# Sparse attention and Fourier mixing: the first attention without conversion, and Strassen in half of the first batch's second layer

## The chip, the cores and the metric

The kernel runs on one core of a Trainium2 chip. The metric is the device time of one execution in microseconds (us). Engines are named as in the profile: PE is the matrix engine (PEld its weight loads), DVE the vector engine, ACT the scalar engine, POOL the general-purpose engine, SP the engine whose queue issues most DMAs.

## What is computed

Attention over 4 batches, 8 heads, 768 tokens, head size 64, with a local window and a summary of every block of 32 tokens; then a Fourier mix, a normalization and two dense layers. Cut to what matters:

```python
k_sum = k.reshape(B, H, nb, 32, D).max(axis=3)          # 24 block summaries
v_sum = v.reshape(B, H, nb, 32, D).mean(axis=3)
local = where(|i - j| < 16, (q @ k.T) / 8, -1e9)
block = (q @ k_sum.T) / 8 + log(32)
a = softmax(concatenate([local, block], -1))
x = (a @ concatenate([v, v_sum], 2))                     # to (4, 768, 512)
u = x + real(fft(fft(x, axis=1), axis=2))
un = (u - mean(u)) / sqrt(var(u) + 1e-6)
out = u + relu(un @ w_ch1) @ w_ch2                       # 512 x 2048, 2048 x 512
```

The two weight matrices arrive as 64-bit floats, which the kernel reads as pairs of 32-bit words and converts on the chip.

## The kernel before

`_main_program` (line 487) handles batches 0 to 3 one after the other: attention (`gen_attention`, 788) in four pairs of heads, Fourier mix (`gen_fourier`, 972), first dense layer (`gen_hidden`, 1086) and second (`gen_out`, 1133). The dense layers go in two halves of four of the eight 128-wide blocks j of each half of the hidden dimension, in the order hidden 0, out 0, hidden 1, out 1. Attention and Fourier mix of the next batch are woven into the dense layers of the present one by `drive` (1220), which steps several generators in turn; a priority is given to the Fourier mix. `_general_program` (78 to 416) runs only if a flag found at the end says that the fast program's numbers were out of bounds.

Strassen's method (in Winograd's form) computes a product of two 2x2 block matrices with 7 block products in place of 8. `_left_sums` (473) and `_right_sums` (480) make the sums that it needs, four each. `gen_hidden` uses it in all batches (line 1101, 384 columns an instruction, right sums of the normalized input, left sums of the weights). `gen_out` uses it for batches 1 to 3 (line 1167, 256 columns, left sums of h in tiles of tag "s"), and for batch 0 the plain product (line 1142, 512 columns). The matmuls are fp32, which PE does in two instructions each.

The weights: `plan` (827) lists pieces (matrix, block j, stage that must have been issued first). `load_raw` (833) loads their words, three ahead, `convert` (847) turns 128x512 of them into floats with five DVE operations (L857, L858, L862, L864 and a product by `tt`, L560) and two ACT operations (L859, L860), `make` (870) does two pieces for a block, for the first matrix its left sums too, and stores the result to DRAM, from where the later batches fetch it (`get_w1` 908, `get_w2` 915). For the second matrix batch 0 stores four parts; batch 1 fetches these, makes the four right sums on DVE and stores parts 1 to 6, and batches 2 and 3 fetch all seven.

The first attention (batch 0 only) is "wide": queries are taken 64 at a time against 96 keys (`wide_scores` 685, L695, L699), the exponentials are multiplied by a mask `wide` of 128 x 768 (the band, and which tokens exist; rows 96 to 119 are the 24 block summaries), and `wide_values` (713, L718) multiplies by `vw`, a tile with a row of values for each of 96 keys, the block sums below, and a column of counts that gives the softmax's sum. `load_wide_values` (625) loads it, with one DMA for a head (two for the first, where the rows before token 0 are left at zero). `prepare` (656) transposes k and q of a pair on PE (L668) and copies them to SBUF (L670 for batch 0, L678 for others), `block_sums` (584) adds up v over each block for two pairs at once (POOL chains by `gtt`, L563; DVE for batch 1, L560 and L605), and `sum_values` (705) brings the sums to `vw` by way of PE (L709) and ACT (L710). The raw data of the block sums are in the tiles of tag "s" as long as weights are being made.

`fetch` (545, L547) issues a DMA on SP's queue, in program order until batch 0's dense layers. What SP waits for holds all that is behind it. DMAs of SP and ACT share eight semaphores in turn, so that each waits for the landing of the one eight places before it.

In `gen_fourier` DVE first makes sums and differences of the two halves of the tokens, for each parity (`sd`, `zw`, `fg`, with small copies to `zq` and the edges of `fg`, L990, L994, L997), PE then multiplies by tables (L1014), and DVE and ACT normalize. `keep_busy` (946, L952) has PE multiply a few idle products while DVE makes the first fold. `tc.issue_after(marks[...])` holds an instruction in the schedule until the marked one.

Of the kernel before, what the change touches and what calls it, by code (L numbers as in the profile page):

```python
# [422 lines left out]
def _tables(S, DM):  # L423

    g = _general_consts(S, DM)
    nb = S // BLOCK

    r, i, c = np.arange(96)[:, None, None], np.arange(S // QB)[None, :, None], np.arange(QB)[None, None, :]
    tok = QB * i - W + r
    wide = np.ones((P, S // QB, QB), dtype=np.float32)  # L430
    wide[0:96] = (r > c) & (r < c + 2 * W) & (tok >= 0) & (tok < S)
    count = np.zeros((P, 1), dtype=np.float32)
    count[0:96], count[96:96 + nb] = 1.0, BLOCK

    r, i, c = np.arange(64)[:, None, None], np.arange(nb)[None, :, None], np.arange(BLOCK)[None, None, :]
    tok = BLOCK * i - W + r
    near = (r > c) & (r < c + 2 * W) & (tok >= 0) & (tok < S)
    near = np.concatenate([near, near]).astype(np.float32)


    sel = np.zeros((4 * nb, 2, 2, 2, 32), dtype=np.float32)
    half = np.zeros((2, 2, 32, 2), dtype=np.float32)
    for h in range(2):
        half[:, h, :nb, h] = 1.0
        for e in range(2):
            for pair in range(2):
                for n in range(nb):
                    sel[(2 * pair + e) * nb + n, pair, e ^ h, h, n] = 1.0

    fs = np.ascontiguousarray(np.moveaxis(g["fs"], 2, 0))  # L450


    fd = g["fd"].reshape(P, 6, DM // 2)
    n = DM // 4
    odd = fd[:, 1, 1:n].copy()
    odd[0] = 0.0
    fm = np.concatenate([fd[:, 0, 0:n + 1], fd[:, 3, 0:n], odd, fd[:, 4, 0:n], fd[:, 1, 0:n + 1]], axis=1)
    fm = np.ascontiguousarray(fm)
    return dict(wide=wide, near=near, sel=sel.reshape(4 * nb, 2, P), half=half.reshape(P, 2), count=count, fs=fs,
                fd=g["fd"], fm=fm, ident=g["ident"])  # L460
# [26 lines left out]
def _main_program(ctx, tc, q, k, v, moe_w_ch1, moe_w_ch2, out):  # L487
# [36 lines left out]
    wide = bpool.tile([P, NC, 2, S], FP, tag="h", name="wide").rearrange("p j h s -> p (j h s)")  # L524
    wide = wide[:, 0:NQ * QB].rearrange("p (n c) -> p n c", n=NQ)
    near = cpool.tile([P, 2, NB2, BLOCK], FP, name="near")
    sel = cpool.tile([4 * nb, 2, P], FP, name="sel")
    half_of = cpool.tile([P, 2], FP, name="half")
    count = cpool.tile([P, 1], FP, name="count")
    rebias = cpool.tile([P, 1], FP, name="rebias")  # L530
# [52 lines left out]

    def block_sums(b, gg):

        f = BLOCK // 4
        n = f * D
        if done_weights:
            raw = room(f"vb_{b}_{gg}")
            raw = [raw[0:4 * nb, n * i:n * (i + 1)] for i in range(4)]  # L590
        else:

            raw = [bpool.tile([P, NC, P], FP, tag="s", bufs=5, name=f"vb_{b}_{gg}_{i}").rearrange("p n t -> p (n t)")
                   [0:4 * nb] for i in range(4)]
        for i in range(4):
            fetch(out=raw[i], in_=v[b, 4 * gg:4 * gg + 4].rearrange("h (n f) d -> (h n) (f d)", f=BLOCK)
                  [:, n * i:n * (i + 1)])
        vb = spool.tile([4 * nb, D], FP, tag="vbs", bufs=2, name=f"vbs_{b}_{gg}")

        add = tt if b == 1 else gtt  # L600
        add(raw[0], raw[0], raw[1], ADD)
        add(raw[2], raw[2], raw[3], ADD)
        add(raw[0], raw[0], raw[2], ADD)
        if b == 1:
            nc.vector.tensor_reduce(out=vb, in_=raw[0].rearrange("p (f d) -> p d f", d=D), op=ADD, axis=AX.X)  # L605
        else:
            while f > 2:
                f //= 2
                gtt(raw[0][:, 0:f * D], raw[0][:, 0:f * D], raw[0][:, f * D:2 * f * D], ADD)
            gtt(vb, raw[0][:, 0:D], raw[0][:, D:2 * D], ADD)  # L610
        sums[b, gg] = vb

# [7 lines left out]
    def load_values(b, g):  # L620
        if g % 2 and following(b, g, 1):
            block_sums(*divmod((b * NP + g + 1) // 2, NP // 2))
        (load_wide_values if is_wide(b) else load_narrow_values)(b, g)

    def load_wide_values(b, g):

        vw = wide_vw(g)
        for e in range(2):
            off = v[b, 2 * g + e].offset
            parts = [(W, WK, 0, NQ), (0, W, 1, NQ)] if (b, g, e) == (0, 0, 0) else [(0, WK, 0, NQ)]  # L630
            for r0, r1, i0, i1 in parts:
                fetch(out=vw[r0:r1, e, i0:i1, 0:D],
                                  in_=bass.AP(v.tensor, off + (QB * i0 - W + r0) * D,
                                              [[D, r1 - r0], [QB * D, i1 - i0], [1, D]]))

    def load_narrow_values(b, g):
# [3 lines left out]
        if g < 2 and is_wide(b - 1):  # L640
            nc.gpsimd.memset(vw[WK:P, :, D:D1], 1.0)
        for e in range(2):
# [42 lines left out]
    def wide_scores(b, g):  # L685
# [3 lines left out]
        for half in range(2):  # L689
# [10 lines left out]
            for e in range(2):  # L700
                nc.scalar.activation(out=p[:, e, n0:n1], in_=ps[e], func=AF.Exp, scale=SC)
                tt(p[:, e, n0:n1], p[:, e, n0:n1], wide[:, n0:n1], ALU.mult)
        return p

    def sum_values(b, g):

        ps = abank([P, 2, D], f"vs_{b}_{g}")
        for e in range(2):
            nc.tensor.matmul(ps[WK:P, e], sel[:, g % 2, D * e:D * e + 32], sums[b, g // 2], start=True, stop=True)  # L709
        nc.scalar.copy(out=wide_vw(g)[WK:P, :, :, 0:D],  # L710
# [43 lines left out]
    def values(b, g, p, pm, x):  # L754
        vw = vw_bufs[g % 2]
        ps = abank([P, D], f"vs_{b}_{g}")
        nc.tensor.matmul(ps, sel[:, g % 2, :], sums[b, g // 2], start=True, stop=True)
        tt(vs[:, :, 0:D], ps[:, None, :].to_broadcast([P, 2, D]),
# [29 lines left out]
    def gen_attention(b):  # L788
        x = bpool.tile([P, NST, DM], FP, tag="x", bufs=2, name=f"x_{b}")
        x_of[b] = x  # L790
        for g in range(NP):
            p = (wide_scores if is_wide(b) else scores)(b, g)
            yield
            if is_wide(b):
                sum_values(b, g)
            else:
                sum_scores(b, g, p[1])
            n1, n2 = following(b, g, 1), following(b, g, 2)
# [3 lines left out]
            if n1:  # L802
                with tc.issue_after(marks["last av"]) if early else ExitStack():
                    prepare(*n1)

            for n in {(0, 1): (), (0, 2): (2,), (0, 3): (2, 3)}.get((b, g), (3,)):
# [4 lines left out]
            if not early:  # L811
                if is_wide(b):
                    wide_values(b, g, p, x)
                else:
                    values(b, g, *p, x)
            if n2:
                load_values(*n2)
            if (b, g) == (0, 0):
                load_raw(2)
            yield  # L820
# [5 lines left out]

    plan = [(1, 0, None), (1, 1, ("fold", 0)), (1, 2, ("mx", 0)), (2, 0, ("mx", 0)), (1, 3, ("h", 0, 0)), (2, 1, ("mx", 0)),
            (2, 2, ("mx", 0)), (2, 3, ("mx", 0)), (1, 4, ("h", 0, 1)), (1, 5, ("h", 0, 2)), (1, 6, ("h", 0, 3)),
# [41 lines left out]
    def make(f, j):  # L870
# [10 lines left out]
        if f == 1:  # L881
            _left_sums(tt, lambda i: wv[:, i])
        else:

            to, wv = to[:, 0:4], wv[:, 0:4]
        yield
        stores.append((to, wv))
# [27 lines left out]
    def get_w2(b, j):  # L915
# [3 lines left out]
        wt[2, b, j] = w  # L919
        if b == 1:  # L920
            fetch(out=w[:, 0:4], in_=dw2[j][:, 0:4])
# [50 lines left out]
    def gen_fourier(b):  # L972
# [10 lines left out]
        for par in range(2):  # L983
# [5 lines left out]
            keep_busy(b, par, zw)  # L989
            nc.vector.tensor_copy(out=zq[:, par], in_=zw[:, :, Q])  # L990
            nc.vector.memset(fg[:, :, Q:Q + 1], 0.0)
            tt(fg[:, :, 1:Q], zw[:, :, 1:Q], zw[:, :, HD - 1:Q:-1], ADD)
            tt(fg[:, :, Q + 1:HD], zw[:, :, 1:Q], zw[:, :, HD - 1:Q:-1], SUB)
            nc.vector.tensor_copy(out=fg[:, :, 0:DM:HD], in_=zw[:, :, 0:DM:HD])  # L994
            tt(fg[:, :, HD + 1:HD + Q], zw[:, :, HD + 1:HD + Q], zw[:, :, DM - 1:HD + Q:-1], SUB)
            tt(fg[:, :, HD + Q:DM - 1], zw[:, :, HD + 1:HD + Q], zw[:, :, DM - 1:HD + Q:-1], ADD)
            ins = nc.vector.tensor_copy(out=fg[:, :, DM - 1:DM], in_=zw[:, :, HD + Q:HD + Q + 1])  # L997
            fgs.append(fg)
# [134 lines left out]
    def gen_out(b, c):  # L1133
        x, h = x_of[b], wt["h", b]
        js = range(NC * c, NC * (c + 1))
        if b == 0:

            for t in range(NST):
# [7 lines left out]
                tt(x[:, t, :], ps, x[:, t, :], ADD)  # L1146
                if NC * (c + 1) == NJ:
                    fetch(out=out[b, P * t:P * (t + 1), :], in_=x[:, t, :])
            issued.add(("o", b, c))
# [46 lines left out]
    load(0, 0)  # L1196
    fetch(out=wide, in_=dr["wide"].ap())
    nc.scalar.dma_start(out=count, in_=dr["count"].ap())
# [3 lines left out]
    for kt, km in zip(kt_bufs, km_bufs):  # L1202
        nc.vector.memset(kt[:, 0:W], 0.0)
        nc.vector.memset(kt[:, W + S:], 0.0)
        nc.vector.memset(km, 0.0)
    nc.vector.memset(vw_bufs[0][0:W, 0, 0:D], 0.0)
    block_sums(0, 0)
    load_values(0, 0)
    load(0, 1)
    prepare(0, 0)  # L1210
    for vw in vw_bufs:
        nc.gpsimd.tensor_copy(out=vw[:, :, D], in_=count.to_broadcast([P, nb]))
    load_values(0, 1)
# [35 lines left out]
    attn = gen_attention(1)  # L1249
    drive((gen_fourier(0), 4, 600), (first(weights, 66), 12, 0), (first(attn, 5), 1, 0))  # L1250
    for b in range(B):

# [66 lines left out]
```

## Time and profile before

| | us |
|---|---|
| median of 6 runs | 848.32 (846.68 to 849.58) |
| profiled execution | 848.45 |
| its span, first to last instruction | 846.7 |
| granted PE clock, mean | 0.987 |
| first attention, to the first fold on DVE | 0 to 57.3 |
| Fourier mix of batch 0, to the first X of layer 1 | 57.3 to 104.5 |
| out, second half of batch 0, with the Fourier mix of batch 1 | 241.2 to 304.6 |
| batches 1, 2, 3 start their layer 1 at | 304, 503, 696 |

The profile's busy shares are in the section on the prediction. The 40 slices of the span show the early part as the only place where PE is not full, and the clock low there (tenths, each slice 21 us):

```profile
PE   5979998999999999999999999999999999999997
DVE  2487996987976443544357943443338953532352
PEclk8969999999999999999999999999999999999999
DMA  9998685979523273444943235403411326205001
```

How to read its lines: a group of instructions gives line, engine, operation, tiles written and read, shape, count, then busy time and mean duration of one in ns, then the idle time before them and what ended it. The chain of waits follows the last instruction back: each row has a start, a length and what took it. A window row gives, for each engine, busy us and in brackets the number of instructions, then the granted clock, the DMA share and GB/s.

### The profile page before, as it was taken

Reading aid. Unit: us, or ns where it says so; the run is one execution under the profiler, and the core shown is the slowest. Engines: PE = TensorE matmul, PEld = TensorE weight load, DVE = VectorE, ACT = ScalarE, POOL = GpSimd, SP = SyncE. Lnnn points to the kernel's source line nnn. Section 1 sums busy time; section 2 is a strip of 40 time slices with the busy share of each in tenths; the row PEclk is TensorE's granted clock in tenths of the full one; section 3 lists DMA queues with packets and bytes.
Section 4 is the critical chain, followed back from the end, with each engine's and each line's share of the span. In section 5 each row is a group of like instructions: output and inputs, shape, how many; then the busy total and the mean of one; then the engine's idle time right before and its main releaser. Section 6 shows DMA issues by size and latency. Waiting matters only on the chain.

```text
span 846.7 us, 14497 instructions
## 1 busy us (share of the span) xinstructions
PE 814.0 (96%) x6006; PEld 568.9 (67%) x6006; DVE 480.4 (57%) x1115; ACT 230.4 (27%) x473; POOL 37.0 (4%) x44
## 2 busy tenths in 40 slices
PE   5979998999999999999999999999999999999997
PEld 4847754545556555787667875688667885786586
DVE  2487996987976443544357943443338953532352
ACT  3524666552721113122232103120321112101100
POOL 3200002003000200001000000000000000000000
PEclk8969999999999999999999999999999999999999
DMA  9998685979523273444943235403411326205001
GB/s 215 230 275 166 156 230 183 260 246 294 205 81 131 75 268 135 120 108 152 249 103 102 73 132 217 111 24 78 171 59 57 113 65 246 87 1 217 1 27 53
DMA packets 102858, 120.94 MB, mean 143 GB/s; under 512 B 50592, under 2 KB 83584, under 8 KB 102784
## 3 DMA queue, kind: packets, MB, share of 16 engines
q1 hardware_dynamic: 102240, 119.77, 48.8%
q8 instruction: 49, 0.80, 0.4%
q10 hardware_dynamic: 544, 0.17, 0.1%
q14 instruction: 25, 0.20, 0.1%
HBM read 95.80 MB, written 24.12 MB: 142 GB/s over the span
## 4 chain that ended last, share of the span: by engine, by line
PE 80%; DVE 9%; ACT 6%; DMA 3%; issue 1%; SPq 0%; ACTq 0%; DVEq 0%
PE hx L1101 18%; PE ox L1167 13%; PE o L1142 9%; PE hz L1101 9%; PE oz L1167 7%; PE hy L1101 4%; PE y L1014 4%; PE oy L1167 3%; DVE x L560 3%; PE sc L735 2%; PE mx L963 1%; ACT qt L678 1%; ACT kt L678 1%; PE sc L695 1%; PE unt L1079 1%
## 5 line engine op out<-in xcount | busy, mean ns | idle before, releaser
L1101 PE MATMUL hx<-u,w 128*128 128x384 f32 x512 | 186.1, 492 | 8.5 <-ACT h L1111 6.5
L1101 PEld LDWEIGHTS hx<-u,w 128*128 128x128 f32 x512 | 94.4, 190 | 75.2 <-ACT h L1111 9.8
L1101 PE MATMUL hz<-u,w 128*128 128x384 f32 x256 | 93.2, 486 | 0.0
L1142 PE MATMUL o<-w,h 128*128 128x512 f32 x192 | 84.9, 595 | 0.0
L1101 PEld LDWEIGHTS hz<-u,w 128*128 128x128 f32 x256 | 48.6, 190 | 33.9 <-ACT h L1118 0.2
L1167 PE MATMUL ox<-w,s 128*128 128x256 f32 x288 | 69.0, 381 | 0.4 <-DVE x L560 0.3
L1167 PE MATMUL oz<-w,s 128*128 128x256 f32 x288 | 68.7, 379 | 0.0
L1167 PE MATMUL ox<-w,h 128*128 128x256 f32 x288 | 66.9, 380 | 0.0
L1142 PEld LDWEIGHTS o<-w,h 128*128 128x128 f32 x192 | 35.7, 190 | 41.9 <-issue 39.9
L560 DVE TENSOR_TENSOR x<-ox,x 128x256 f32<-128x256 f32 x72 | 30.3, 423 | 55.7 <-PE ox L1167 55.7
L1167 PEld LDWEIGHTS ox<-w,h 128*128 128x128 f32 x288 | 54.4, 190 | 8.3
L1167 PEld LDWEIGHTS ox<-w,s 128*128 128x128 f32 x288 | 53.9, 190 | 8.4 <-DVE x L560 1.2
L1167 PEld LDWEIGHTS oz<-w,s 128*128 128x128 f32 x288 | 54.4, 190 | 7.2
L560 DVE TENSOR_TENSOR h<-hx,h 128x384 f32<-128x384 f32 x32 | 17.8, 556 | 71.5 <-PE hx L1101 71.5
L560 DVE TENSOR_TENSOR h<-hy,h 128x384 f32<-128x384 f32 x32 | 17.8, 556 | 57.2 <-PE hy L1101 54.0
L1111 ACT COPY h<-hx 128x384 f32<-128x384 f32 x32 | 15.3, 478 | 121.7 <-PE hx L1101 110.0
L1101 PE MATMUL hy<-u,w 128*128 128x384 f32 x128 | 46.5, 486 | 0.0
L1127 ACT ACTIVATE h<-hx 128x384 f32<-128x384 f32 x32 | 15.7, 491 | 78.9 <-PE hx L1101 78.8
L1014 PE MATMUL y<-fs,fold 128*128 128x193 f32 x192 | 37.1, 336 | 0.0
L679 DVE TENSOR_REDUCE km<-kt 128x24 f32<-128x768 f32 x16 | 15.2, 952 | 38.5 <-ACT kt L678 25.1
L1014 PEld LDWEIGHTS y<-fs,fold 128*128 128x128 f32 x192 | 31.1, 189 | 7.6 <-issue 6.0
L1101 PEld LDWEIGHTS hy<-u,w 128*128 128x128 f32 x128 | 24.3, 190 | 17.0
(125 smaller groups left out, 1105.4 us busy)
## 6 DMA issues: line engine op xcount, KB each, us to landing
w<-dw SPq DMA_DIRECT2D x40, 896.0 KB, 5.2
words<-in_moe_w_ch_dram SPq DMA_DIRECT2D x32, 512.0 KB, 6.6
vw<-in_v_dram SPq DMA_DIRECT2D x47, 192.0 KB, 5.8
dw<-w SPq DMA_DIRECT2D x8, 896.0 KB, 7.1
kn<-in_k_dram SPq DMA_DIRECT2D x16, 384.0 KB, 4.8
qn<-in_q_dram SPq DMA_DIRECT2D x16, 384.0 KB, 5.4
vb<-in_v_dram SPq DMA_DIRECT2D x32, 192.0 KB, 5.5
out_dram<-x SPq DMA_DIRECT2D x24, 256.0 KB, 2.6
```

Of the source, the lines that this page charges most:

```text
L560: nc.vector.tensor_tensor(out=out, in0=in0, in1=in1, op=op)
L678: nc.scalar.copy(out=dst[D * e:D * (e + 1), s:S:2], in_=ps[D * s:D * (s + 1)])
L679: nc.vector.tensor_reduce(out=km[:, 0:nb], in_=kt[:, W:W + S].rearrange("p (n f) -> p n f", f=BLOCK), op=ALU.max, axis=AX.X)
L695: nc.tensor.matmul(ps[e][0:WK, n - n0, :], kt[rows, QB * n:QB * n + WK], qt[rows, QB * n:QB * (n + 1)], start=True, stop=True)
L735: nc.tensor.matmul(ps[h][r:r + 64, i, :], kt[rows, o:o + 64], qt[rows, o:o + BLOCK], start=True, stop=True)
L963: nc.tensor.matmul(out, y[:, g], table, start=True, stop=last, skip_group_check=True)
L1014: nc.tensor.matmul(y, fgs[par][:, st, P * g:P * (g + 1)], fs[par][:, g % 2, st, :], start=(st == 0), stop=(st == HT - 1))
L1101: nc.tensor.matmul(ps, w[:, a, kk, :], u[:, r, kk, :], start=start and kk == 0, stop=stop and kk == 1, skip_group_check=True)
L1111: nc.scalar.copy(out=c11, in_=X)
L1127: nc.scalar.activation(out=c21, in_=X, func=AF.Relu)
L1142: nc.tensor.matmul(ps, h[:, n, hf, P * t:P * (t + 1)], wt[2, b, j][:, 2 * hf:2 * hf + 2, :], start=(n, hf) == (0, 0), stop=(n, hf) == (NC ...
L1167: nc.tensor.matmul(ps, left[a][:, n, :], wt[2, b, j][:, r, :], start=start and n == 0, stop=stop and n == NC - 1, skip_group_check=True)
```

## The change

It has eight parts.

1. The mask becomes one pattern of 128 x 64, broadcast over the tiles of queries; what is out of range is handled by zeroed value rows and zero counts (now 128 x 12). Both are loaded by ACT's queue. `vw` is loaded with three DMAs a head.
2. Two products of zeros on PE stand before the first transposes, after a memset on POOL.
3. `block_sums` of batch 0's first two pairs are done pair by pair (48 rows). Those of batch 1's first two pairs move from DVE to POOL; those of its last two stay on DVE and move behind the Fourier mix of batch 0.
4. The sums of pair 0 are brought to `vw` after the transposes of pair 1, no longer before them.
5. The first piece of the weights waits for the fold of batch 0, and so leaves the first attention; `load_raw(2)` moves ahead of a pair's value loads.
6. In `gen_out` the second half of batch 0 goes by Strassen, as in later batches.
7. For that, batch 0 makes the right sums of blocks 4 to 7 of the second matrix and stores all seven parts, and batch 1 fetches them.
8. Small copies in `gen_fourier` (three for each parity, all batches) go from DVE to ACT, and the mark "fold" moves to the product that is now last.

```diff
@@ tables
-    wide = np.ones((P, S // QB, QB), dtype=np.float32)
-    wide[0:96] = (r > c) & (r < c + 2 * W) & (tok >= 0) & (tok < S)
-    count = np.zeros((P, 1), dtype=np.float32)
-    count[0:96], count[96:96 + nb] = 1.0, BLOCK
+    wide = np.ones((P, QB), dtype=np.float32)
+    wide[0:96] = (r > c) & (r < c + 2 * W)
+    count = np.zeros((P, S // QB), dtype=np.float32)
+    count[0:96] = (QB * i - W + r >= 0) & (QB * i - W + r < S)
+    count[96:96 + nb] = BLOCK
@@ block_sums
-    def block_sums(b, gg):
+    def block_sums(b, gg, g=None):
+        rows, heads = (4 * nb, slice(4 * gg, 4 * gg + 4)) if g is None else (2 * nb, slice(2 * g, 2 * g + 2))
...
-        add = tt if b == 1 else gtt
+        add = tt if (b, gg) == (1, 1) else gtt
@@ load_values
-        if g % 2 and following(b, g, 1):
+        if g % 2 and following(b, g, 1) and (b, g) != (1, 1):
             block_sums(*divmod((b * NP + g + 1) // 2, NP // 2))
@@ load_wide_values
-            parts = [(W, WK, 0, NQ), (0, W, 1, NQ)] if (b, g, e) == (0, 0, 0) else [(0, WK, 0, NQ)]
+            parts = [(W, WK, 0, 1), (0, WK, 1, NQ - 1), (0, WK - W, NQ - 1, NQ)]
@@ wide_scores
-                tt(p[:, e, n0:n1], p[:, e, n0:n1], wide[:, n0:n1], ALU.mult)
+                tt(p[:, e, n0:n1], p[:, e, n0:n1], wide[:, None, :].to_broadcast([P, NQ // 2, QB]), ALU.mult)
@@ gen_attention
-            if is_wide(b):
+            if not is_wide(b):
+                sum_scores(b, g, p[1])
+            elif g:
                 sum_values(b, g)
-            else:
-                sum_scores(b, g, p[1])
...
                     prepare(*n1)
+            if (b, g) == (0, 0):
+                sum_values(b, g)
...
+            if (b, g) == (0, 0):
+                load_raw(2)
             if n2:
                 load_values(*n2)
-            if (b, g) == (0, 0):
-                load_raw(2)
@@ plan, make, get_w2, gen_out
-    plan = [(1, 0, None), (1, 1, ("fold", 0)), ...
+    plan = [(1, 0, ("fold", 0)), (1, 1, ("fold", 0)), ...
...
+        elif j < NC:
+            to, wv = to[:, 0:4], wv[:, 0:4]
         else:
-            to, wv = to[:, 0:4], wv[:, 0:4]
+            _right_sums(tt, lambda i: wv[:, i])
...
-        if b == 1:
+        if b == 1 and j < NC:
             fetch(out=w[:, 0:4], in_=dw2[j][:, 0:4])
...
-        if b == 0:
+        if (b, c) == (0, 0):
@@ gen_fourier
-            nc.vector.tensor_copy(out=zq[:, par], in_=zw[:, :, Q])
+            nc.scalar.copy(out=zq[:, par], in_=zw[:, :, Q])
...
-            nc.vector.tensor_copy(out=fg[:, :, 0:DM:HD], in_=zw[:, :, 0:DM:HD])
+            nc.scalar.copy(out=fg[:, :, 0:DM:HD], in_=zw[:, :, 0:DM:HD])
...
-            ins = nc.vector.tensor_copy(out=fg[:, :, DM - 1:DM], in_=zw[:, :, HD + Q:HD + Q + 1])
+            nc.scalar.copy(out=fg[:, :, DM - 1:DM], in_=zw[:, :, HD + Q:HD + Q + 1])
@@ start
-    fetch(out=wide, in_=dr["wide"].ap())
+    zeros = bpool.tile([P, 7, 2, S2], FP, tag="u", name="zeros").rearrange("p a k n -> p (a k n)")[:, 0:640]
+    nc.gpsimd.memset(zeros, 0.0)
+    ps = bank([P, 512], "warm")
+    for i in range(2):
+        nc.tensor.matmul(ps, zeros[:, 512:640], zeros[:, 0:512], start=True, stop=True)
+    nc.scalar.dma_start(out=wide, in_=dr["wide"].ap())
...
-    nc.vector.memset(vw_bufs[0][0:W, 0, 0:D], 0.0)
-    block_sums(0, 0)
+    for g in range(2):
+        nc.vector.memset(wide_vw(g)[0:W, :, 0, 0:D], 0.0)
+        nc.vector.memset(wide_vw(g)[64:WK, :, NQ - 1, 0:D], 0.0)
+    block_sums(0, 0, 0)
     load_values(0, 0)
     load(0, 1)
+    block_sums(0, 0, 1)
     prepare(0, 0)
@@ main schedule
     drive((gen_fourier(0), 4, 600), (first(weights, 66), 12, 0), (first(attn, 5), 1, 0))
+    block_sums(1, 1)
```

## The prediction

> **What bounds the kernel now.** I read the busy shares first, then the costliest groups, then the chain of waits, then stages.
>
> ```profile
> PE 814.0 (96%) x6006; PEld 568.9 (67%) x6006; DVE 480.4 (57%) x1115; ACT 230.4 (27%) x473; POOL 37.0 (4%) x44
> PE 80%; DVE 9%; ACT 6%; DMA 3%; issue 1%; SPq 0%; ACTq 0%; DVEq 0%
> L1142 PE MATMUL o<-w,h 128*128 128x512 f32 x192 | 84.9, 595 | 0.0
> L1167 PE MATMUL ox<-w,s 128*128 128x256 f32 x288 | 69.0, 381 | 0.4 <-DVE x L560 0.3
> ```
>
> TensorE (PE) is busy nearly always and 80% of the chain, so a saved PE instruction counts wherever PE does not pause. L1142 is the plain second layer of batch 0, L1167 the Strassen one of the later batches. Their means overlap, so I take rates from runs on the chain (start us, us, what):
>
> ```profile
> 283.34 21.46 PE o L1142 x50
> 742.37 3.45 PE ox L1167 x16
> ```
>
> A 512-wide instruction costs 21.46/50 = 0.429 us, a 256-wide one 3.45/16 = 0.216 us. Windows then show whether PE and DVE have room where batch 0's second half runs (PE busy, PEld, DVE, ACT, POOL, clock, DMA share, GB/s):
>
> ```profile
> 240.00:250.00 10.00, 10.00 (x31) 4.95 (x29) 9.12 (x16) 1.03 (x3) 0.00 (x0) 1.00 0.12 34
> 260.00:270.00 10.00, 10.00 (x62) 7.83 (x62) 8.17 (x27) 0.00 (x0) 0.00 (x0) 1.00 0.27 93
> 290.00:300.00 10.00, 10.00 (x25) 4.46 (x24) 1.38 (x2) 0.00 (x0) 3.18 (x4) 1.00 0.13 45
> ```
>
> PE is full there; DVE is not (the six windows from 240 to 300 hold 37.0 us of DVE work, 23 idle). The first attention is the opposite. The chain begins and ends in waits there:
>
> ```profile
> 9.34 8.73 DMA kn<-in_k_dram
> 18.21 4.81 PE qk L668 x48
> ...
> 52.90 0.60 DVE vb L560
> 53.65 0.92 DVE vbs L605
> ...
> 55.04 0.60 DVE words L862
> 55.74 0.57 DVE words L864
> 56.78 0.60 DVE w L560
> 57.37 1.68 DVE fold L560
> ```
>
> Pair 1's keys land at 18.1 while PE has stood still; the transposes behind run at half clock (the windows from 16 to 22 grant 0.50). At the end, DVE finishes block sums of batch 1 and a weight conversion before it may start the first fold. Three queue rows, for the place of pair 2's keys (start, time held, what):
>
> ```profile
> 16.83 1.65 SPq L547 DMA_DIRECT2D vw<-in_v_dram  x2
> 18.57 4.18 SPq L547 DMA_DIRECT2D kn<-in_k_dram  x1
> 21.43 1.27 POOL L563 TENSOR_TENSOR vb<-vb,vb 96x512 f32<-96x512 f32 x1 [4.34 <-DMA vb<-in_v_dram]
> ```
>
> **The change part by part.**
>
> Strassen in the second half of batch 0's second layer. It removes 6 tiles x 8 products of 512 columns; fp32 takes 2 instructions each: 96 x 0.429 = 41.2 us. It adds 3 x 7 x 4 x 2 = 168 of 256 columns: 168 x 0.216 = 36.2. **-5.0 us.** The groups' means (0.442 over 192 from 84.9; (69.0+68.7+66.9)/864 = 0.237) would give 42.4 - 39.8 = -2.6: the other bound. I take the chain's rates, since those are spans of consecutive work. DVE pays 12 left sums at 0.69 (a 128x512 operation), 21 updates at 0.42 and loses 6 at 0.69: +13 us, hidden by the 23 idle ones. Without that cover PE would wait; the same layout in batches 1 and 2 makes PE wait 0.3 us in all (the L1167 row). The right sums of four weight blocks (16 x 0.42 = +6.7) fall into 210 to 240, where DVE is busy 22.8 of 30: 7.2 idle, a tight fit. If they spill, the fold of batch 1, at 241, is late by what spills (0 to 2). The larger stores (+393 KB four times) go on queues with a share of 0.4 to 0.8.
>
> In batch 1 the same 16 sums and four stores vanish. PE lost at most 0.4 us there against batch 2: -0.2 (0 to -0.4).
>
> Start of the first attention. Less is loaded before pair 1's keys: the mask goes from 384 to 33 KB, the block-sum data of the first group is halved (-0.39 MB): 0.74 MB at the 0.24 MB/us of these windows is 3 us, so landing at 15 instead of 18.1. PE's pause before it then falls from 3.5 us (13.66 to 17.14) to about 1.4. But the value sums of pair 0 now come after these transposes: PE copies 0.4 to PSUM, ACT spreads them in 1.43, and the value products wait, 1.8 us that lay beside other work before. Scores of pair 1 (24.39 before) start at 15 + 4.8 + 1.8 + 1.44 = 23.0 at half clock, at 21.1 at full (2.9 for the transposes): **about -2**. The two warm-up products cost four instructions at 0.86, 3.4 us, after a memset on the idle POOL, ahead of keys that land at 4.78: nothing, as the next thing late is pair 1's load; without that cover a few tenths. Four memsets on DVE and the count copies on POOL lie in idle time too.
>
> Pair 2's keys. On SP they used to be issued at 18.57, behind two value loads. Now there stand before them: four block-sum loads of 96 KB for pair 1 (each waits for the sums of pair 0 on POOL, which free its buffers), four loads for batch 1, of which the last waits for the third sum of pair 1's chain on POOL, and six value loads instead of two. SP also holds each DMA until the one issued eight places earlier has landed, as the program's semaphores go round (so SP waits 1.7 us on `sel`, which ACT loads), and keys 2 wait for a load of batch 1. POOL's first chain (six sums of 48x512; 6 us in the 96x512 rows) ends about 16, the third sum of the second about 21; add the 5.5 us median landing of such loads: keys 2 leave about 25.5 at the latest and land after 4.8 (their median), at 30.3; with landings of 3 us, at 28. I take 29.5. PE, ready at about 26.6, starts them 0.9 later than the 28.60 of before. So start and keys together: **+0.9**, from -2.0 (landing in time) to +4 (30.8 and half a clock, which cost 4.81 - 2.9 = 1.9 at pair 1).
>
> The Trainium skill (TensorE: Matmul & The Clock Gate, Part 1) says an idle window of about 3.4 us halves the clock, and its closing table asks for no pause over 3 us. Its rule would charge nothing for my pause of 2.9 and some 1.7 more for one half a microsecond longer. The 3.48 us pause above is followed by 0.50, which agrees.
>
> End of the first attention. Block sums of batch 1 (0.60, 0.92) and conversion steps (0.60, 0.57, 0.60) leave DVE's last stretch, 3.29 us. The limit becomes the last value products, 54.71 by the records, plus a reciprocal and a product: fold at 55.4 instead of 57.3: **-1.9** (0 to -3.3).
>
> Fold stage. Four left sums (4 x 0.41) and six small copies, which go to an idle ACT, leave it, so the first mixed half comes 1.7 sooner. But the conversion removed from the attention returns behind it (+4.9), against -0.6 copies, -2.7 block sums moved on, -0.9 conversion moved on, -1.2 end of attention, +0.9 batch-1 scores: +0.4 on a DVE busy for 40.7 of the 45.5 us up to layer 1. I take **0** (-1.7 to +0.4). In the first layer 1, DVE takes the late block sums (2.7; the first tiles wait for DVE and ACT there: 0 to +2), and ACT's first copy of a product stands ahead of four q copies of 0.5 (-2 to 0): **0**. Extra mask broadcasts and batch 0's later value loads (6 per pair) I cost at nothing, covered by PE's work from 28 to 50.
>
> Sum: -5.0 - 0.2 + 0.9 - 1.9 + 0 = -6.2. The profiled execution is 848.45 (span 846.7 and 1.75 around it), the median 848.32: 842.25, stated as **842.2 us**.
>
> A rule against the change: the Trainium skill (DMA: Bandwidth & Descriptors, Anatomy of one DMA) gives each DMA a fixed 2.0 us whatever its size, in a fit for another issuing path. By it the 14 more DMAs through eight places would cost at most an estimated 14 x 2/8 = 3.5 us, and the sum would be 845.7. Here 1 KB of `half` took 6.83 us to land in a full queue, so queueing, not the fixed part, sets it.
>
> **The rivals.**
>
> *The early part pays in full.* Keys 2 land by 26.6 (-2.0 instead of +0.9), and the fold's 1.7 reaches layer 1. For: less is loaded, and small loads may land in 3 us. Against: the waits on SP. 842.2 - 2.9 - 1.7 = 837.6.
>
> *SP's queue loses it all (slower).* If the second block-sum data of pair 1 land at 21 to 23, as batch 1's did (the POOL row: 21.43, next load 22.89), POOL's third sum ends at 25.5, batch 1's load lands at +7.2, the median of the early loads, 32.7, and keys 2 at about 36.5: 7.9 later than the use at 28.60, plus 1.9 of half clock: +9.8 in place of +0.9: 851.1. It decides once keys 2 land after about 34: slower than before needs +6.2 on top of +0.9. For: DMA engines are saturated until 60. Against: those bytes were issued 3 us earlier.
>
> *Strassen's gain does not arrive.* Right sums spill past 241, batch 1's fold and x updates are late, and PE waits: -2.6 at best, +2 spilled: 842.2 + 2.4 + 2.0 = 846.6. Against: 7.2 idle against 6.7, and batches 1 and 2.
>
> **How the numbers follow.** Forecast (839.5 to 845.5) 0.52; early part in full 0.16; Strassen lost 0.15; SP's queue 0.17. 0.2% (1.7 us) is what a measurement of this kernel tells from none. Of "Strassen lost" 0.07 is same, 0.08 faster; of SP's queue 0.15 slower and 0.02 same. Faster 0.52 + 0.16 + 0.08 = 0.76, same 0.09, slower 0.15. The range takes the forecast, nearly all of the Strassen case and most of the early gain: 837.5 to 848.0.
>
> **What would show it.** Right: 168 instructions of 256 columns between about 235 and 300 at 0.216 and no PE pause there; keys 1 landing near 15; vs and ACT's spreading before the first av; fold near 56.3. PE idle before the third transposes shows the keys' price: none means the first rival, over 6 us the second. The prediction is wrong if PE waits in out(0,1), or if the clock stays low through the first attention; if hidden(0,0) starts more than 3 us away from 104.5, the wash on DVE was wrong.

## The result and the profile after

The changed kernel takes 855.03 us (median of 17 runs, 848.45 to 863.35) against 848.04 for the kernel before: the ratio is 1.0072, 95% interval 1.0055 to 1.0088. It is slower; 842.2 was forecast. The comparison leaves out the executions above 1.5% of the fastest, which is why the ratio stands below that of the medians. The times spread with the granted clock: of the executions on record, the ten with a mean clock of 0.985 to 0.993 took 848 to 856 us, the nine others (0.970 to 0.979) 859 to 863. The profiled one is of the second kind: 860.6, span 858.7, clock 0.976.

The page after, busy shares, chain and the two forms of the second layer:

```profile
PE 826.5 (96%) x6082; PEld 595.3 (69%) x6082; DVE 491.3 (57%) x1117; ACT 233.4 (27%) x497; POOL 48.7 (6%) x57
...
PE 81%; DVE 10%; ACT 5%; DMA 2%; issue 1%; SPq 1%; ACTq 0%
...
L1174 PE MATMUL ox<-w,s 128*128 128x256 f32 x336 | 80.7, 381 | 0.3
...
L1151 PE MATMUL o<-w,h 128*128 128x512 f32 x96 | 43.9, 612 | 0.9 <-DVE w L560 0.9
```

Half of L1142 (192 instructions, now L1151 with 96) has become L1174, as intended, and PE hardly waits there (0.3). Yet PE is busy 12.5 us longer, with fewer columns to multiply: time went to a slower clock. Up to 840 us the profile grants half clock for 20.5 us before and for 41.0 us after. By stage, from the first instruction of each in the two profiled executions:

| stage | before | after | difference | forecast |
|---|---|---|---|---|
| start to pair 2's transposes | 28.60 | 30.07 | +1.5 | +0.9 |
| from there to the first fold | 28.70 | 34.15 | +5.4 | -1.9 |
| fold to first hidden half of batch 0 | 47.16 | 49.04 | +1.9 | 0 |
| first to second hidden half | 100.36 | 105.71 | +5.3 | 0 |
| second hidden half to batch 1 (Strassen) | 99.81 | 96.08 | -3.7 | -5.0 |
| batch 1, first to second hidden half | 88.18 | 92.09 | +3.9 | -0.2 |
| from there to batch 2, and to the end | 453.89 | 451.56 | -2.3 | 0 |
| span | 846.70 | 858.70 | +12.0 | -6.2 |

Five stages lost. Not forecast either is the gain of 2.3 in the last row but one: 0.9 and 0.6 lie in the stretches with the Fourier mixes of batches 2 and 3, 0.8 behind the start of the last hidden half, and no run isolates the cause. PE's timeline after (start, length, instructions, in brackets the idle time before and what ended it):

```profile
14.68 2.57 PE L670 MATMUL qk<-ident,kn 128*64 128x128 f32 x24 [2.52 <-DMA kn<-in_k_dram]
30.07 2.83 PE L670 MATMUL qk<-ident,kn 128*64 128x128 f32 x24 [3.12 <-DMA kn<-in_k_dram]
...
150.57 2.02 PE L1110 MATMUL hx<-u,w 128*128 128x384 f32 x4 [2.08 <-DVE h L560]
...
215.00 0.94 PE L776 MATMUL av<-vs,p 64*128 64x130 f32 x12 [2.14 <-DVE vs L560]
...
325.03 2.40 PE L1110 MATMUL hx<-u,w 128*128 128x384 f32 x4 [2.08 <-DVE h L560]
```

Before, no pause between 60 and 560 us was over 1.83; here, besides the pause for the fold (2.68 at 66.04), three are over 2. Four 384-wide instructions last 2.02 and 2.40 behind them instead of 1.45. The first of the three stands behind DVE operations that POOL's additions held up, here a mask product that takes 0.55 us alone:

```profile
146.10 1.62 DVE L560 TENSOR_TENSOR p<-p,near 128x384 f32<-128x384 f32 x1
144.07 3.23 POOL L563 TENSOR_TENSOR vb_None<-vb_None,vb_None 96x512 f32<-96x512 f32 x2 [2.28 <-DVE h L560]
```

SP's queue and the windows of the first attention say why the keys are late and what a pause costs (window rows: PE, PEld, DVE, ACT, POOL, clock, DMA share, GB/s):

```profile
14.36 7.37 SPq L547 DMA_DIRECT2D vb_None<-in_v_dram  x4
21.78 4.36 SPq L547 DMA_DIRECT2D vw<-in_v_dram  x6
26.23 0.39 SPq L547 DMA_DIRECT2D kn<-in_k_dram  x1
```

```profile
30.00:32.00 2.00, 1.93 (x18) 1.96 (x20) 0.28 (x1) 0.00 (x0) 0.45 (x1) 0.50 1.22 290
...
52.00:54.00 2.00, 2.00 (x7) 0.65 (x7) 0.00 (x0) 0.00 (x0) 0.00 (x0) 0.50 1.01 414
54.00:56.00 2.00, 2.00 (x15) 1.67 (x15) 1.53 (x4) 0.86 (x2) 1.31 (x2) 0.50 1.00 400
```

Pair 2's keys leave at 26.2 behind block sums that nobody needs yet, and the 48 transposes after the pause run at half clock. From 49.1 to 62.8 the clock is at half once more, as it was before from 49.6; but now PE is busy in 13.3 of these 13.7 us and DVE in 4.2, so PE's half speed is the attention's end. Before, DVE was the busy one there, 2.00 of 2 us from 52 on:

```profile
56.00:58.00 2.00, 0.00 (x0) 0.00 (x0) 2.00 (x4) 0.00 (x0) 0.00 (x0) 0.50 1.41 141
```

### The profile page after: what moved, and what is told of

The parts are those of the page before. It is cut to its first block, busy times and chain, and to the rows that moved or that the text cites. A ratio compares the mean times of both kernels' runs of the same rounds, so it can differ in the third digit from the quotient of the medians.

```text
span 858.7 us, 14724 instructions
## 1 busy us (share of the span) xinstructions
PE 826.5 (96%) x6082; PEld 595.3 (69%) x6082; DVE 491.3 (57%) x1117; ACT 233.4 (27%) x497; POOL 48.7 (6%) x57
## 4 chain that ended last, share of the span: by engine, by line
PE 81%; DVE 10%; ACT 5%; DMA 2%; issue 1%; SPq 1%; ACTq 0%
PE hx L1110 17%; PE ox L1174 16%; PE hz L1110 8%; PE oz L1174 8%; PE hy L1110 4%; PE y L1023 4%; PE oy L1174 4%; PE o L1151 3%; PE sc L738 2%; DVE w L560 2%; PE mx L971 2%; DVE x L560 2%; ACT kt L680 1%; PE unt L1088 1%; PE qk L670 1%; ACT qt L680 1%
## 5 line engine op out<-in xcount | busy, mean ns | idle before, releaser
L1174 PE MATMUL ox<-w,s 128*128 128x256 f32 x336 | 80.7, 381 | 0.3
L1174 PE MATMUL oz<-w,s 128*128 128x256 f32 x336 | 80.5, 379 | 0.0
L1174 PE MATMUL ox<-w,h 128*128 128x256 f32 x336 | 78.0, 380 | 0.0
L560 DVE TENSOR_TENSOR x<-ox,x 128x256 f32<-128x256 f32 x84 | 35.3, 423 | 60.9 <-PE ox L1174 60.9
L1174 PEld LDWEIGHTS ox<-w,h 128*128 128x128 f32 x336 | 63.5, 190 | 9.6
L1174 PEld LDWEIGHTS ox<-w,s 128*128 128x128 f32 x336 | 62.9, 190 | 9.3 <-DVE x L560 1.1
L1174 PEld LDWEIGHTS oz<-w,s 128*128 128x128 f32 x336 | 63.6, 190 | 8.3
L1151 PE MATMUL o<-w,h 128*128 128x512 f32 x96 | 43.9, 612 | 0.9 <-DVE w L560 0.9
L1174 PE MATMUL oy<-w,h 128*128 128x256 f32 x168 | 39.7, 379 | 0.0
```

The source lines that it names most:

```text
L560: nc.vector.tensor_tensor(out=out, in0=in0, in1=in1, op=op)
L1151: nc.tensor.matmul(ps, h[:, n, hf, P * t:P * (t + 1)], wt[2, b, j][:, 2 * hf:2 * hf + 2, :], start=(n, hf) == (0, 0), stop=(n, hf) == (NC ...
L1174: nc.tensor.matmul(ps, left[a][:, n, :], wt[2, b, j][:, r, :], start=start and n == 0, stop=stop and n == NC - 1, skip_group_check=True)
```

## The experiments

All times are medians; the ratio is to the kernel before, with its 95% interval. "Fold", "first" and "second" are the starts of the first fold and of the two hidden halves of batch 0 in the profiled execution; "pair 2" is the start of its transposes.

| run | us | ratio | interval |
|---|---|---|---|
| without Strassen | 853.86 | 1.0091 | 1.0055 to 1.0127 |
| Strassen only | 847.90 | 0.9999 | 0.9980 to 1.0018 |
| Strassen, sums deferred | 846.59 | 0.9981 | 0.9965 to 0.9997 |
| SP order | 848.38 | 0.9999 | 0.9983 to 1.0015 |
| + conversion back | 852.35 | 1.0042 | 1.0019 to 1.0065 |
| + late block sums on POOL | 851.27 | 1.0037 | 1.0025 to 1.0050 |
| + right sums on POOL | 845.06 | 0.9968 | 0.9954 to 0.9982 |
| + all three | 853.80 | 1.0054 | 1.0034 to 1.0074 |
| right sums on POOL, batch 2's sums on DVE | 843.33 | 0.9931 | 0.9906 to 0.9956 |
| right sums on POOL, memset off POOL | 844.66 | 0.9959 | 0.9940 to 0.9979 |
| before + Strassen, right sums on POOL | 843.70 | 0.9944 | 0.9924 to 0.9963 |
| changed kernel again | 856.11 | 1.0084 | 1.0053 to 1.0116 |
| combined | 840.96 | 0.9913 | 0.9882 to 0.9944 |
| combined, keys 1 first | 834.94 | 0.9844 | 0.9811 to 0.9878 |
| before, batch 2's sums on DVE | 845.31 | 0.9969 | 0.9953 to 0.9985 |

**Which half of the change loses.**

```diff
 # changed kernel: gen_out, make and get_w2 as before
-        if (b, c) == (0, 0):
+        if b == 0:
```

> The changed kernel with the second half of batch 0's second layer plain again (and its right sums back in batch 1). Theory: the loss is early (first attention and the layers of batch 0 up to the second hidden half: +14.2 us in the profiled execution), Strassen itself gave 4.1 us and cost 3.0 at the start of batch 1, where DVE waits for w2: about 856, with layer 1 of batch 1 starting some 4 us later than in the changed kernel's profile and no PE pause at its 6th tile. Rival, the second layer is the culprit: back to 848 or less.

853.86, and no pause at batch 1's sixth tile. Fold 59.34, second hidden half 102.97 after the first. The net loss is early, not in the second layer; and with Strassen (855.03) or without, the changed kernel takes the same within the intervals, since what Strassen gains (3.7) batch 1 loses (3.9). Layer 1 of batch 1 starts at 311.78, not 4 us behind the 315.05 of the changed kernel, as this profile is of an execution at a clock of 0.991.

```diff
 # kernel before: gen_out, make and get_w2 as in the changed one
-        if b == 0:
+        if (b, c) == (0, 0):
```

> The kernel before with only the Strassen half (its right sums in batch 0, all seven parts stored, batch 1 fetching them for blocks 4 to 7). Theory: 848.0 - 4.1 + 3.0 = about 847, first attention unchanged (fold near 57.3), a PE pause of about 3 us early in batch 1 where DVE waits for w2 from DRAM. Rival: the 16 right sums hold DVE in the second hidden half, 849 or more; second rival, the early parts are harmless and this is the loss: 855.

847.90: second hidden half to batch 1 takes 95.83 instead of 99.81, a gain of 4.0, and the first attention and the stages up to there are as before (second minus first 100.16). Batch 1 then takes 89.71 between its hidden halves instead of 88.18, with a pause of 1.27 on DVE's `h`. The right sums do not hold PE; the time did not move, though, by anything that the interval could show, and some 1.5 us of the gain went to a longer end, which from the start of the last update on takes 5.2 to 7.5 in the different runs and stays unexplained.

**The pause in batch 1.** In the chain of waits of the changed kernel:

```profile
316.13 6.80 DMA w<-dw
...
322.95 0.44 DVE w L560
...
323.42 0.49 DVE w L560 x2
...
324.43 0.56 DVE h L560
...
325.03 2.40 PE hx L1110 x4
```

DVE stands at the right sums of w2 until their load has landed; the sum that PE needs for its next tile, `h`, is behind them. The load is late as its buffer is: the last tile of the plain layer reads block after block, for some 6.9 us (16 x 0.429), so the first block's buffer comes free well ahead of the end; SP began to issue these loads at 299.68, 5 us ahead of batch 1's first tile at 304.63, and DVE's first sums ran at 303.44. In Strassen's order every product, the last one too, reads all four blocks; the loads leave at 313.95 and 316.13 with the first tile at 315.05.

```diff
-            _right_sums(tt, lambda i: w[:, i])
...
+            if b == 1 and j < NC:
+                w2 = wt[2, b, j]
+                _right_sums(tt, lambda i: w2[:, i])
```

> As the Strassen half alone, but in batch 1 the right sums of blocks 0 to 3 are issued on DVE after the block's own tiles and no longer ahead of them. Theory: the wait of DVE for w2 no longer stands ahead of the tiles that PE needs: no pause, 848.0 - 4.1 = about 844. Rival, the pause comes from the late buffers or the DMA queue itself and not from DVE's order: 847 as the Strassen half alone.

846.59, with the pause at 308.97 (1.97). The edit did not do what it was to do: in the trace DVE's sums of w2 still stand ahead of `h`, since the scheduler, not the place in the code, sets DVE's order (four `w` sums from 306.89, `h` at 308.36). The run tells nothing of the theory.

```diff
-            _right_sums(tt, lambda i: w[:, i])
+            _right_sums(gtt, lambda i: w[:, i])
```

> The SP-order kernel with batch 1's right sums of blocks 0 to 3 on POOL. Theory: the late w2 loads hold DVE's queue, not PE's own data; with the sums elsewhere the pause of 2.26 at the sixth tile of batch 1 goes, and the first hidden half of batch 1 to the second takes 88.2 as before instead of 90.7: about 846. Rival: the pause stays, since the loads delay something else: 848.

845.06; the pause is gone and batch 1 takes 88.20 between its hidden halves, to 0.02 what it took before. That DVE's queue was the holder is shown. (The stage ahead, first to second hidden half of batch 0, took 107.61, not 104.51; more on it below.)

The same edit on the kernel with Strassen only:

> The kernel before with the Strassen half and batch 1's right sums of blocks 0 to 3 on POOL. Theory: it adds to the Strassen half alone (847.9) what the same edit gave on the SP-order kernel (3.3 of 848.4, of which 2.4 in batch 1): 845 to 845.8, no pause of PE on DVE early in batch 1. Rival: batch 1's pause returns elsewhere: 847.5 or more.

843.70, below the 845 expected: with this edit the Strassen half alone is worth 4.3 us, where it was worth nothing. The profiled execution is the slowest of this run (850.29, clock 0.979), but batch 1 takes 88.21 between its hidden halves in it, without the pause.

**SP's order.**

```diff
+    load(0, 2)
     load_values(0, 1)
-    load(0, 2)
 # and in load_values, for (0, 1) alone
+            load_wide_values(b, g)
             block_sums(*divmod((b * NP + g + 1) // 2, NP // 2))
-            load_wide_values(b, g)
```

> The changed kernel with pair 2's keys and queries, then pair 1's values, ahead of batch 1's block-sum loads on SP's queue. Theory: the 3.1 us pause before pair 2's transposes and the half clock behind it (30 to 35.5, 2.6 us) go: fold some 5 us sooner, about 849.5 to 851. Rival, the pause moves to pair 1's value loads or the clock falls anyway later: 854 to 856.

848.38, 6.6 below the changed kernel's median and some 4.5 below its ten executions of the better clock (median 852.8). Keys 2 leave at 14.37, pair 2 starts at 28.21 with no pause, and the fold comes at 54.05, 3.3 sooner than before the change. Between 20 us and the pause for the fold no half clock appears. What is left is behind the fold: first hidden half +49.7 (47.16 before), second +104.5 (100.36 before).

**The work that left the first attention.**

```diff
-    plan = [(1, 0, ("fold", 0)), (1, 1, ("fold", 0)), ...
+    plan = [(1, 0, None), (1, 1, ("fold", 0)), ...
```

> The SP-order kernel with the first weight piece converted in the first attention again. Theory: between the fold and the second hidden half DVE is the limit, so the conversion moved there (4.9 us of DVE) costs what it lasts: the second hidden half starts 3 to 5 us earlier after the fold than in the SP-order run (154.2 us), while the fold comes 0 to 2 later than 54.05: about 845. Rival, the wash that was forecast holds and the delay is from another move: 848 to 849.

852.35, a miss. Fold to first hidden half falls to 45.56, 4.2 less than in the SP-order run. That is at most the conversion's price there, where 0 was forecast for all moves: up to 1.7 of it can be a step of 3.4 us of half clock at 94.8 that only the SP-order run has, and the first hidden half itself starts at 104.04, no sooner than the 103.78 of that run. For the fold comes at 58.48: PE pauses for DVE at 44.94 (1.53), the clock is at half from 45.7 to 66.2, and later a pause of 4.09 at 207 costs another half clock. So neither place is free.

```diff
-        add = tt if (b, gg) == (1, 1) else gtt
+        add = gtt
```

> The SP-order kernel with the block sums of batch 1's last two pairs on POOL at the same place (2.7 us less for DVE in the first hidden half). Theory of a DVE limit: the second hidden half 2 to 2.7 earlier after the fold than 154.2: about 846. Rival: DVE has room there, or POOL at work slows DVE's own operations as much: 848 to 849.

851.27: DVE has less to do and the second hidden half comes later (107.30 after the first, not 104.51), with POOL adding nearly without a break from 125.7 to 140.5. The theory that the amount of DVE work sets this stage fell here; its rival, POOL at work slowing DVE, was next.

The edits of these two runs and the right sums on POOL, together:

> All three edits at once on the SP-order kernel. Theory: the gains add, 848.4 - 3.5 - 2.4 - 2.4 = about 840 to 842, since the first two relieve one queue and the third another place. Rival: once DVE is relieved, PE takes over and only the largest counts: 844 to 846.

853.80: the losses of the first two hide the gain of the third (88.20 between batch 1's hidden halves). The three single effects would add up to 851.9.

**POOL beside DVE.** The kernel before shows it, in lines that were in reach of the prediction. DVE's timeline, and POOL's at the same time:

```profile
190.50 0.69 DVE L862 SCALAR_TENSOR_TENSOR words<-words 128x512 int32<-128x512 int32 x1 [0.29 <-ACT words L859]
191.11 0.68 DVE L864 SCALAR_TENSOR_TENSOR words<-words 128x512 f32<-128x512 uint32 x1
...
192.91 1.53 DVE L862 SCALAR_TENSOR_TENSOR words<-words 128x512 int32<-128x512 int32 x1 [0.45 <-ACT words L859]
194.37 1.75 DVE L864 SCALAR_TENSOR_TENSOR words<-words 128x512 f32<-128x512 uint32 x1
196.04 0.68 DVE L560 TENSOR_TENSOR x<-o,x 128x512 f32<-128x512 f32 x1
```

```profile
192.63 1.27 POOL L563 TENSOR_TENSOR vb<-vb,vb 96x512 f32<-96x512 f32 x1 [60.61 <-DVE words L858]
194.13 3.12 POOL L563 TENSOR_TENSOR vb<-vb,vb 96x512 f32<-96x512 f32 x2 [0.23 <-DMA vb<-in_v_dram]
197.32 1.92 POOL L563 TENSOR_TENSOR vb<-vb 96x256 f32<-96x256 f32 x2
```

The same two instructions take 0.69 and 0.68 alone, 1.53 and 1.75 with POOL at work; `x<-o,x`, with one operand in PSUM, keeps its 0.68.

```diff
+        on_dve = (b, gg) in ((1, 1), (2, 0), (2, 1))
-        add = tt if (b, gg) == (1, 1) else gtt
+        add = tt if on_dve else gtt
```

> The SP-order kernel with batch 1's right sums on POOL (845.06), and batch 2's block sums on DVE instead of POOL. Theory: while POOL adds, DVE's operations beside it take two to three times as long (0.55 us become 1.6 at 133 to 138), which makes the pauses of 2.04 at 139.6 and 2.13 at 204.7, each followed by half a clock; with the sums on DVE (2.7 us each) both pauses go or fall under 1.5, the first hidden half to the second takes 103 or less instead of 107.6: 840 to 843. Rival: DVE has no room for 5.5 us more, same or slower: 845 or more.

843.33. DVE has 5.5 us more to do, and the second hidden half starts 99.44 after the first instead of 107.61; the pauses of 2.04 and 2.13 are gone (the largest left in this stage is 0.95), and no half clock stands in it. The median moved by 1.7 only, with intervals that just touch, though eight of its nine executions lie below the fastest of the twelve without the edit. In the profiles the first hidden half starts 3.3 later (105.60, not 102.29), behind 6.8 us of half clock from 92.8 on that the other profile has not. Two views of the timelines of the run without this edit, and with it:

```profile
135.12 1.62 DVE L560 TENSOR_TENSOR p<-p,near 128x384 f32<-128x384 f32 x1
...
139.58 2.93 PE L1113 MATMUL hx<-u,w 128*128 128x384 f32 x4 [2.04 <-DVE h L560]
```

```profile
140.26 0.54 DVE L560 TENSOR_TENSOR p<-p,near 128x384 f32<-128x384 f32 x1
```

```diff
 # kernel before
-        add = tt if b == 1 else gtt
+        on_dve = b == 1 or (b == 2 and not done_weights)
+        add = tt if on_dve else gtt
```

> The kernel before with batch 2's block sums (two chains of some 7 us on POOL at 124 and 193) on DVE. Theory of POOL slowing DVE beside it: DVE gains at 124 to 132 and 193 to 201, first to second hidden half 98 to 99.5 instead of 100.4, time 846.5 to 847.8 against 847.9. Rival: DVE's 5.5 us of added work cost as much as POOL's company: same or slower.

845.31, a larger gain than expected: 2.4 to 2.7 by either median of the kernel before (847.72 beside it, 848.04 above), with nothing else touched, and the second hidden half 97.68 after the first instead of 100.36. From 124 to 132 and from 185 to 199 none of DVE's L863 and L865 (L862 and L864 above) takes over 0.69. The effect is one of POOL beside DVE and not of the moved work.

```diff
-            nc.gpsimd.memset(vw[:, :, D:D1], 1.0)
+            nc.vector.memset(vw[:, :, D:D1], 1.0)
```

> The SP-order kernel with batch 1's right sums on POOL (845.06), and the memset of the narrow value tile on DVE. Theory: POOL's chain for batch 1 no longer waits behind that memset for PE (14 us idle ahead of 47.9) and so no longer runs beside the last mask products (1.3 us each instead of 0.55): fold 1 to 2 sooner than 53.9, 843 to 844.5. Rival: DVE's own queue waits for PE at the memset, or the chain still runs late: 845 to 846.

844.66, with the fold at 51.95 instead of 53.93; the median moved by 0.4 only, not clear of its interval, and the first hidden half starts at 103.25 instead of 102.29: the sooner fold is given back there. Both this edit and batch 2's sums on DVE:

> Both edits that helped on top of the SP-order kernel with batch 1's right sums on POOL: batch 2's block sums on DVE (843.3) and the memset off POOL (844.7). Theory: they relieve two places, the layers of batch 0 and the end of the first attention, and add: 841 to 842.5, fold near 52, second hidden half some 99.5 after the first. Rival: DVE is full between them, and the sooner fold is given back before the first hidden half: 843 to 844.

840.96: fold 52.54, second hidden half 98.97 after the first. The two single effects would give 842.9; the interval holds that, and it overlaps that of batch 2's sums on DVE alone, so that they add is likely but not clear of the noise.

**Pair 1's keys.**

```diff
-    load_values(0, 0)
     load(0, 1)
+    load_values(0, 0)
```

> The combined kernel with pair 1's keys and queries ahead of pair 0's value loads on SP's queue. Theory: the pause before pair 1's transposes (3.4 us, and the half clock behind it) goes, pair 1's transposes start near 13 instead of 16.6: 1 to 3 us below the combined kernel. Rival: pair 0's values then come late for the first value products, or pair 2's keys do: no change.

834.94, 6.0 below the combined kernel where 1 to 3 were expected, and 1.6% below the kernel before. Pair 1's transposes start at 12.84 without a pause, the clock stays at full from there to the pause for the fold, and the fold comes at 48.47:

```profile
12.84 1.53 PE L674 MATMUL qk<-ident,kn 128*64 128x128 f32 x24
14.20 1.48 PE L674 MATMUL qk<-ident,qn 128*64 128x128 f32 x24
```

24 transposes take 1.53 here and took 2.57 behind the pause of 2.52.

**The spread.** The changed kernel, unedited:

> The changed kernel once more. Theory: its executions differ by the granted clock in the first attention: one with mean clock 0.987 or more has no half clock from 49 to 62, its fold comes near 59 instead of 64.2 and it ends near 853; one near 0.976 repeats the first profile with 859 to 861. Rival: the spread comes from elsewhere, and the fold stands at 64 in an execution of 853.

856.11, and the profiled execution was again one of 0.976: fold 64.14, the same pauses (2.07, 2.12, 2.04). No profile of the better group came out, so the fold of an execution of 853 was not seen. What speaks for the theory is the run without Strassen, the same up to the fold: its profile has no half clock from 34.3 to 61.6 and its fold at 59.34, and its executions fall into 852.4 to 853.9 (0.989 to 0.991) and 860.1 to 860.6 (0.979 to 0.981). Why the clock falls near 49 us in some executions and not in others, with no idle of 0.6 us in the ten us ahead of it, stays open. It fell in the kernel before too, where it cost nothing: the Strassen half alone had no fall there and its fold at 56.92, the kernel before a fall from 49.6 and its fold at 57.30.

## Why the prediction was wrong

-6.2 was forecast, and the median rose by 7.0. Strassen's term and the times of the first loads came out; four other steps did not.

**Strassen** (-5.0): the mechanism was right and DVE's cover held. It measured -4.0 (-3.7 in the changed kernel). The right sums fitted into the idle DVE time as argued. The size lies between the rate of the chain, which was taken, and that of the group means (-2.6).

**Batch 1** (-0.2): wrong in sign, +1.5 with Strassen alone and +3.9 in the changed kernel, half clock included. The step asked what the removed sums were worth and not when the buffers of the loads that remain come free: the kernel before issued them 5 us ahead of need. In Strassen's order of reading these buffers come free later, so the loads came late and held DVE's queue, and DVE held PE.

**Start and keys** (+0.9): the times were right. Keys 1 were used at 14.68 (forecast 15), pair 1's scores at 22.81 (21.1 to 23.0), pair 2's transposes at 30.07 after a pause of 3.12 (29.5 after 2.9). The failure is the choice among the ends: full clock behind the pause was taken, and half clock came. Pair 2's scores start at 35.67 against 32.11, +3.6, near the upper bound of +4. The Trainium skill (TensorE: Matmul & The Clock Gate, Part 1) names a window of about 3.4 us; the pauses here that brought half clock were shorter, 2.04 among them, so the measurement decides against the limit used. The prediction read the 3.48 us pause of the kernel before as agreeing with that limit; yet in this profile the clock is full from 13.66, where the pause begins, to 15.46 and at half from there on, after 1.8 us of it.

**End of the attention** (-1.9): right where the clock stays up. From pair 2's transposes to the fold it took 28.70 before, 25.84 in the SP-order run. In the changed kernel it took 34.15. The step read the DVE work at the end as the only limit and did not ask what else that work covered: PE was at half clock from 49.6 in the kernel before as well, and once DVE's conversion and sums left, PE's slow products became the end. Whether the clock falls there at all differs from execution to execution, so the size of this loss is partly bad luck: in the run without Strassen, where it does not fall, the stretch took 28.33.

**Fold to the second hidden half** (0): this is the step that failed most, +7.2 here and +6.7 in the SP-order run. It balanced amounts of DVE work against 4.8 us of idle time and took work on POOL as free of DVE. What the runs showed in its place: DVE's operations last two to three times as long beside POOL's additions, and the pauses of PE that come of it pass 2 us and bring half clock. Of the stage from the first to the second hidden half (+5.3) this is shown: without POOL's sums for batch 2 both pauses go, and it takes 99.44 instead of 107.61. These sums ran on POOL in the kernel before too, where they cost 2.7 (100.36 against 97.68); what is new is that they fall on operations that PE soon waits for, and which move brought them there no run isolates. From the fold to the first hidden half (+1.9) the cause is argued only: the conversion that was moved there (up to 4.2), and 3.4 us of half clock at 103.7. A warning was in the profile before, and was not used: of the sixteen mask products of the first attention (mean 726 ns) the eleven alone took 0.52 to 0.56, the five that ran beside POOL 0.69 to 1.61.

**The rivals.** The slower one had the place right: undoing SP's order gives back 6.6 us, about as much as was lost, but the losses behind the fold and in batch 1 stay and only Strassen's gain covers them. Its price (851.1) was too small and its condition wrong: it was to decide from keys that land after 34, and they landed at 29.9. What made it dear in the profiled execution was the clock, twice (6.8 us of half clock from 28.6, 13.7 from 49.1), more than the wait. That Strassen's gain does not arrive was right too, by another way than the one described. The early part in full did not come with SP's order alone (pair 2 at 28.21, the first hidden half at 103.78); it came, and more, with pair 1's keys first as well (24.92, and 97.54 instead of 104.46). That the combined kernel's 840.96 lies near the forecast of 842.2 is in part luck: it holds batch 2's sums on DVE, which were no part of the change.

## What to carry to other kernels

When work is taken out of a stage, list what it covered: a slow clock or a late load beside it becomes the new end. Order a DMA queue by the time at which each load is needed, and look at when the buffers come free if a loop's order of reading changes. In these profiles a pause of the matrix engine of little more than 2 us mostly costs more by up to an estimated 1.7 us (half of 3.4 us of half clock), and one just under 2 us only itself.

## What the runs showed of the hardware

POOL's additions of two tensors in SBUF and DVE's operations on two tensors in SBUF hold each other up: 0.69 became 1.53 and 0.55 became 1.62, two of POOL's took 3.12 where the one just before took 1.27, while DVE's operations with an operand in PSUM kept their 0.54 (h) and 0.68 (x). The Trainium skill (SBUF — State Buffer, SBUF: two separate sides) says that the port pair which both share is locked for a whole instruction, also by a DVE operation with two SBUF inputs against a POOL operation that reads SBUF; that agrees with these rows.

Of the pauses of PE between 60 and 560 us in the profiles of the first twelve runs and of the two kernels, none of 1.97 us or less was followed by half clock; of fifteen from 2.04 to 2.26, eleven were; all of 2.68 and more were. The clock record says why the fifteen differ. In each profile it changes on a fixed grid of 3.413 us (half clock lasted 3.41, 6.83, 13.65 us), and in these profiles every grid step that holds 2.02 us or more of PE's idle time (fifteen too) was followed by a step at half clock. The four pauses that were not followed (2.13 to 2.26) lay across two steps, with at most 1.61 in one. Steps with 1.8 to 1.9 us of idle time went both ways.

There is an exception: from 88 to 104 us half clock came in ten of all the profiles behind pauses of 0.6 us at most, with 0.8 to 1.2 us of idle time in the step before, among the small products of batch 1's attention (64x32 and 64x65). What the clock counts as idle there, and near 49 us, is open.
